# A planner with prices for VectorE beside GpSimd, ten staging tiles, another order of the first loads, and no idle matmuls

## The chip, the core and the metric

The kernel runs on one core of one Trainium2 chip. The core has TensorE (PE: matmuls; PEld: its weight loads), VectorE (DVE), ScalarE (ACT), GpSimd (POOL) and SyncE (SP), whose queue issues nearly all DMA transfers of this kernel. Each engine runs its instructions in the order in which they are written; an instruction that waits holds up all that stand behind it on its engine. The metric is the time of one execution in device microseconds, lower is better.

## What is computed

Chunked attention over 4 batches, 8 heads, 768 positions and 64 values each, followed by a gated feed-forward layer:

```python
for c in range(nc):                       # 24 chunks of 32 queries
    # keys of the chunk, 16 before, 8 behind, and 8 memory keys
    scores = scale * matmul(q_c, k_full.T)
    a = softmax(scores)
    out[:, :, c_start:c_end] = matmul(a, v_full)
x = out in [B, S, H * D]                  # 4 x 768 x 512
h = maximum(x @ w_in, 0.0)                # 512 -> 1024
u, v = h[..., :512], h[..., 512:]
v_n = (v - mean(v)) / sqrt(var(v) + 1e-6)
v_s = einsum('ts,bsd->btd', w_spatial, v_n) + b_spatial
return (u * v_s) @ w_out                  # 512 -> 512
```

## The kernel before

**A planner writes the order.** The program first lists its operations with `plan.op(engine, us, ...)`: an engine, a price in us, the keys it reads and writes, and a rank. `Plan.order` then simulates the engines with these prices: again and again it takes, over all engines, the operation that could start first, and among those of one engine with equal start the lowest rank. Ring sizes (`sizes`) bound how many tiles of a name are alive. What comes out is one fixed order for each engine; the prices and ranks are used for nothing else.

**First phase, to about 227 us.** 24 units `i` of four chunks go through `attend(i)`: copies of the keys to `kmain` (L377, ScalarE), a burst on TensorE (L395) of scores S(i) into half 0 of `sx` and of value products A(i) of unit i − 1 into half 1, 16 matmuls per pair of heads each; then the maximum `mx` (L445), the subtraction into `p` (L449), the exponential (L453, ScalarE), the sum `den` and its reciprocal `rec` (L458–L461); the transposes of `p` into `pt` (L475) and of the normalised values `xs` (L430) into `xt` (L490). `xt` is split into a high part (L495, ScalarE, a cast to fp32r) and a low part (L499, VectorE, the difference). `sx`, `p`, `xs` and `pT` have one buffer each. Values come with four transfers per unit into `vmain`.

Between the units stand the matmuls of the feed-forward layer, each product as three (high by high, low by high, high by low, L528–L530): `ffn_v` (512 wide, twelve per 128 positions), then `ffn_u` (384 wide, twelve per block). The v half is normalised and written to DRAM (`vn_far`), the u half too (`u_far`).

**w_in** arrives as 64-bit floats, in eight pieces (c, part) of 128 x 512, each over one of four `big` buffers: ScalarE scales (L824, L829), VectorE shifts (L833, L834), POOL adds (L839), ScalarE casts the high part (L853), VectorE or POOL subtracts the low part (L857). Part 1 serves v, part 0 serves u. w_out's and w_spatial's pieces go the same or a like way later. SP issues all these loads in program order where `seq=True`, and SP also waits there for a free buffer.

**Idle matmuls.** `keep_warm` puts four 512-wide matmuls (L543) on TensorE as soon as the first high part of w_in is there; their result is not used.

**Second phase.** For each batch b, `spatial(b)` multiplies v_n by w_spatial and `ffn_o(b)` multiplies the gated result by w_out, both as a product of seven steps instead of eight (`product`): sums and differences of quarters `sm` (L651, VectorE), high parts `op` (L664, ScalarE), low parts (L667, VectorE), blocks of matmuls (L689; L683 adds the bias), results taken to SBUF (L731, L780), joined (L737) and gated with u (L745, POOL). Both are generators that yield after each step: `spatial` goes p1 p2 p6 p5 p7 p4 p3, `ffn_o` p1 p6 p5 p7 p4 p3 p2. The loop over b takes one step of spatial(b), then ffn_o(b − 1), then the rest of spatial(b).

## Time and profile before

| what | value |
|---|---|
| median of 3 runs | 395.51 us (395.07 to 395.77) |
| profiled execution, its span | 395.85 us, 394.1 us |
| TensorE busy | 368.4 us, 93%, 3428 matmuls |
| VectorE busy | 281.0 us, 71% |
| ScalarE busy | 210.2 us, 53% |
| GpSimd busy | 157.5 us, 40% |
| DMA over the span | 64.93 MB, 165 GB/s |
| chain that ended last | 80% on TensorE, 8% on VectorE |

Busy times are of one profiled execution; the span runs from the first to the last recorded instruction. In a timeline row, the bracket at the end gives how long the engine had been idle and what released it. A row of a transfer on SP's queue gives when it was issued.

### The profile page before, as it was taken

To read this page: it belongs to the slowest core of one execution; us is meant where nothing else is said; L and a number is where in the kernel's file an instruction comes from. 1 tells how busy PE (TensorE), PEld (TensorE's weight loads), DVE (VectorE), ACT (ScalarE), POOL (GpSimd) and SP (SyncE) were. 2 spreads that over 40 slices of the span, in tenths; PEclk is the share of its full clock that TensorE was granted. 3 is DMA by queue.
4 is the path that set the end of the run, shared out by engine and by line. 5 is a ranking of instruction groups with operands and counts; after the bars stand their busy time and mean duration, and the time that the engine had idled before them with its cause. 6 is when DMAs were issued, how large, how long until landed. Compare 5 with 4: busy or idle time off the path is not lost.

```text
span 394.1 us, 8707 instructions
## 1 busy us (share of the span) xinstructions
PE 368.4 (93%) x3428; PEld 335.0 (85%) x3428; DVE 281.0 (71%) x465; ACT 210.2 (53%) x368; POOL 157.5 (40%) x161
## 2 busy tenths in 40 slices
PE   1659899999999999999999998899999999999996
PEld 1437688898898988988889898799999999999996
DVE  7975965756856558866575499978956794788594
ACT  4765646575456557464434475438434734473361
POOL 8433762193621177601012968770226033403520
PEclk9999999999999999999999999999999999999999
DMA  8998567676575683786603768403640562040014
GB/s 231 309 232 210 129 202 230 183 251 185 182 219 160 235 221 112 211 223 206 187 29 136 257 237 278 136 25 121 210 153 0 162 233 89 0 175 27 2 40 161
DMA packets 47356, 64.93 MB, mean 165 GB/s; under 512 B 4434, under 2 KB 38866, under 8 KB 47316
## 3 DMA queue, kind: packets, MB, share of 16 engines
q1 hardware_dynamic: 46900, 64.25, 53.5%
q8 instruction: 27, 0.44, 0.5%
q10 hardware_dynamic: 416, 0.13, 0.1%
q14 instruction: 13, 0.11, 0.1%
HBM read 45.49 MB, written 18.87 MB: 163 GB/s over the span
## 4 chain that ended last, share of the span: by engine, by line
PE 80%; DVE 8%; issue 2%; ACT 2%; POOL 1%; ACTq 0%
PE y L689 16%; PE f L689 12%; PE f L528 12%; PE sx L395 11%; PE f L530 11%; PE f L529 11%; PE xt L490 3%; PE pt L475 3%; DVE wout L857 2%; DVE sm L651 2%; DVE op L667 2%; POOL ug L745 1%; DVE st L737 1%; ACT op L664 1%; DVE st L834 0%
## 5 line engine op out<-in xcount | busy, mean ns | idle before, releaser
L745 POOL TENSOR_TENSOR ug<-st,ug 128x384 f32<-128x384 f32 x32 | 43.8, 1380 | 79.6 <-DVE st L737 62.0
L528 PE MATMUL f<-x,win_h 128*128 128x384 f32 x128 | 45.8, 358 | 0.0
L574 POOL TENSOR_TENSOR rstd<-ve,mhalf 128x1 f32<-128x1 f32 x24 | 13.5, 562 | 77.4 <-DVE ve L570 75.7
L664 ACT CAST op<-sm 128x768 fp32r<-128x768 f32 x32 | 26.3, 837 | 32.5 <-DVE sm L651 29.9
L530 PE MATMUL f<-x,win_h 128*128 128x384 f32 x128 | 43.2, 338 | 0.0
L529 PE MATMUL f<-x,win_l 128*128 128x384 f32 x128 | 43.0, 336 | 0.0
L528 PE MATMUL f<-win_h,x 128*128 128x512 f32 x96 | 41.6, 433 | 0.0
L689 PE MATMUL y<-wsp,op 128*128 128x384 f32 x192 | 39.5, 341 | 2.0 <-ACT st L731 1.2
L395 PE MATMUL sx<-kmain,q 128*32 128x128 f32 x768 | 28.5, 294 | 11.3 <-ACT kmain L377 9.3
L377 ACT COPY kmain<-k 64x640 f32<-64x640 f32 x48 | 34.7, 724 | 6.8 <-DMA k<-in_k_dram 4.0
L530 PE MATMUL f<-win_l,x 128*128 128x512 f32 x96 | 38.2, 398 | 0.0
L529 PE MATMUL f<-win_h,x 128*128 128x512 f32 x96 | 38.1, 397 | 0.0
L430 DVE TENSOR_TENSOR xs<-sx,rec 128x512 f32<-128x512 f32 x24 | 16.6, 690 | 29.7 <-PE sx L395 29.7
L667 DVE TENSOR_TENSOR op<-sm,op 128x768 fp32r<-128x768 f32 x32 | 33.6, 1056 | 5.3 <-ACT op L664 4.9
L689 PE MATMUL y<-wout,op 128*128 128x256 f32 x288 | 36.2, 280 | 0.8 <-ACT ot L780 0.7
L395 PEld LDWEIGHTS sx<-kmain,q 128*32 128x32 f32 x768 | 21.5, 117 | 18.2 <-POOL vmain L369 10.1
L689 PEld LDWEIGHTS y<-wsp,op 128*128 128x128 f32 x192 | 33.9, 188 | 3.2 <-ACT st L731 1.9
L689 PEld LDWEIGHTS y<-wout,op 128*128 128x128 f32 x288 | 34.9, 188 | 1.2 <-ACT ot L780 0.9
L369 POOL COPY vmain<-memv 8x1024 f32<-8x1024 f32 x22 | 23.8, 1083 | 17.6 <-PE sx L395 16.2
L689 PE MATMUL f<-wsp,op 128*128 128x384 f32 x144 | 29.4, 339 | 1.5 <-DVE op L667 1.5
L599 ACT ACTIVATE uo<-f 128x384 f32<-128x384 f32 x32 | 15.6, 490 | 26.8 <-PE f L530 17.7
L689 PE MATMUL f<-wout,op 128*128 128x256 f32 x216 | 27.3, 280 | 0.0
(100 smaller groups left out, 833.4 us busy)
## 6 DMA issues: line engine op xcount, KB each, us to landing
vmain<-in_v_dram SPq DMA_DIRECT2D x48, 128.0 KB
vn_far<-st SPq DMA_DIRECT2D x24, 256.0 KB
u_far<-uo SPq DMA_DIRECT2D x32, 192.0 KB
vr<-vn_far SPq DMA_DIRECT2D x8, 768.0 KB
ug<-u_far SPq DMA_DIRECT2D x16, 384.0 KB
q<-in_q_dram SPq DMA_DIRECT2D x11, 512.0 KB
out_dram<-ot SPq DMA_DIRECT2D x36, 128.0 KB
vmain<-in_v_dram SPq DMA_DIRECT2D x47, 96.0 KB
```

What stands on the lines that cost most here:

```text
L369: {"DVE": nc.vector, "POOL": nc.gpsimd}[eng].tensor_copy(to, of)
L377: nc.scalar.copy(kmain[i % NK][rows, :, r, :, 0:CH], k_of(i)[rows].rearrange("p t (c s) -> p t c s", s=CH))
L395: nc.tensor.matmul(o, w_, m, start=True, stop=True, skip_group_check=True)
L430: nc.vector.tensor_tensor(xs, t_["sx", i][:, 1], rec.unsqueeze(3).broadcast_to([P, T, 2, D]), op=ALU.mult)
L528: nc.tensor.matmul(o, lh, rh, start=(j == 0), stop=False)
L529: nc.tensor.matmul(o, ll, rh, start=False, stop=False)
L530: nc.tensor.matmul(o, lh, rl, start=False, stop=(j == len(pairs) - 1))
L599: op("ACT", act(HT), lambda: nc.scalar.activation(alloc("uo", i, [P, HT], F32), t_["f", n], AF.Relu), r=[("f", n)], w=[("uo", i)], rank=rank)
L664: nc.scalar.copy(half(0), of())
L667: nc.vector.tensor_tensor(half(1), of(), half(0).bitcast(F32), op=ALU.subtract)
L689: nc.tensor.matmul(o, x, y, start=first and m == 1 and not (seed and bank != "x"), stop=m == 3 * chunks, skip_group_check=True)
L745: nc.gpsimd.tensor_tensor(g, t_[st(x)], g, op=ALU.mult)
```

## The change

The planner gets a flag `shared` on VectorE operations with two inputs in SBUF. Such an operation that starts while POOL is busy is priced longer, by up to a factor of 1.75, and a POOL operation that starts beside a flagged one by up to 1.4. Some prices are set anew. The ring `st` has ten tiles instead of eight. The first values and the second pair of queries and keys are loaded between the w_in pieces; the four part-0 pieces come last with ranks 15 to 18, and their low parts go to VectorE instead of POOL. The four idle matmuls are gone. In the second phase, batches 1 and 2 take two steps of `spatial(b)` before `ffn_o(b - 1)` starts.

```diff
@@ class Plan @@
-    def op(self, eng, us, fn, r=(), w=(), rank=0.0, mb=0.0, tail=0.0, after=None, alone=False, drag=1.0):
+    def op(self, eng, us, fn, r=(), w=(), rank=0.0, mb=0.0, tail=0.0, after=None, alone=False, drag=1.0, shared=False):
...
-        lone = 0.0
+        lone = both = 0.0
...
+            beside, pace = {"DVE": (free["POOL"] if shared else 0.0, 1.75), "POOL": (both, 1.4)}.get(e, (0.0, 1.0))
+            if beside > t:
+                us += min((beside - t) * (1 - 1 / pace), us * (pace - 1))
...
+            if shared:
+                both = t + us
@@ the rings @@
-    sizes = {"f": 3, "sx": 1, "pt": 2, "xt": 1, "y": 5, "st": 8, "big": 4, "uo": 2, "x": 2, "vm": 3,
+    sizes = {"f": 3, "sx": 1, "pt": 2, "xt": 1, "y": 5, "st": 10, "big": 4, "uo": 2, "x": 2, "vm": 3,
@@ burst, softmax, flip, ffn_v @@
-                us += 0.7
+                us += 0.88 if "s" in what else 0.6
-        op("DVE", dve(512) + 0.36, den, r=[("p", i)], w=[("rec", i)], rank=rank + 0.6)
+        op("DVE", dve(512) + 0.43, den, r=[("p", i)], w=[("rec", i)], rank=rank + 0.6, shared=True)
-            op("PE", 0.45, turn, r=[("p", i)], w=[("pt", i)], rank=rank, tail=0.25)
+            op("PE", 0.47, turn, r=[("p", i)], w=[("pt", i)], rank=rank, tail=0.25)
...
-        op("DVE", 1.05, stat, r=[k_], w=[("ve", i)], rank=rank)
+        op("DVE", 1.08, stat, r=[k_], w=[("ve", i)], rank=rank, shared=True)
@@ idle matmuls @@
-    def keep_warm(c, passes, rank):
-
-        n = ("w", c)
-
-        def go():
-            o = alloc("f", n, [P, DH], F32, psum=True)
-            for _ in range(passes):
-                nc.tensor.matmul(o, win_h[:, c, DH:DH + P], win_h[:, c, DH:], start=True, stop=True)
-        op("PE", passes * 0.43, go, r=[("win", c, 1, "h")], w=[("f", n)], rank=rank, tail=0.25)
...
-        if i == 0:
-            for c in range(1):
-                keep_warm(c, 4, 50.0 + c)
@@ product: total, left; split @@
-            op(sum_eng, dve(W) if sum_eng == "DVE" else pool_(W), go, r=keys, w=[sm], rank=rank)
+            op(sum_eng, dve(W) if sum_eng == "DVE" else pool_(W), go, r=keys, w=[sm], rank=rank,
+               shared=sum_eng == "DVE")
-            op("DVE", dve(W), low, r=[*keys, (*ok, "h")], w=[(*ok, "l")], rank=rank)
+            op("DVE", dve(W), low, r=[*keys, (*ok, "h")], w=[(*ok, "l")], rank=rank, shared=True)
...
@@ the order of the first loads @@
     w_in_part(0, 1, 5.0 + 0, 2.0 + 0, "DVE")
     w_in_part(1, 1, 5.0 + 1, 2.0 + 1, "DVE")
-    w_in_part(2, 1, 5.0 + 2, 2.0 + 2, "DVE")
-    w_in_part(3, 1, 5.0 + 3, 2.0 + 3, "DVE")
     load_v(0)
     load_qk(1)
-    w_in_part(0, 0, 25.0 + 0, 15.0 + 0, "POOL")
+    w_in_part(2, 1, 5.0 + 2, 2.0 + 2, "DVE")
     load_v(1)
-    w_in_part(1, 0, 25.0 + 1, 15.0 + 1, "POOL")
+    w_in_part(3, 1, 5.0 + 3, 2.0 + 3, "DVE")
     load_v(2)
-    w_in_part(2, 0, 25.0 + 2, 15.0 + 2, "POOL")
-    w_in_part(3, 0, 25.0 + 3, 15.0 + 3, "POOL")
+    w_in_part(0, 0, 15.0 + 0, 15.0 + 0, "DVE")
+    w_in_part(1, 0, 15.0 + 1, 15.0 + 1, "DVE")
+    w_in_part(2, 0, 15.0 + 2, 15.0 + 2, "DVE")
+    w_in_part(3, 0, 15.0 + 3, 15.0 + 3, "DVE")
@@ the second phase @@
             spatials.append(spatial(b))
-            next(spatials[b])
+            for _ in range((1, 2, 2, 1)[b]):
+                next(spatials[b])
```

Names in the rows below: an engine's rows are line, operation, destination, sources and shape; lines of the changed kernel are shifted by about five (L395 is now L400, L528 L533, L667 L663, L857 L853).

TensorE, the third to the ninth group of its work, before (`pt` and `xt` are transposes, `kmain` rows are scores, `vmain` rows value products, `f` rows with `x` the v products):

```order
L475 MATMUL pt<-ident,p 128x128 x4
L543 MATMUL f<-win_h 128x512 x4
L395 MATMUL sx<-vmain,pT 32x128 x16
L475 MATMUL pt<-ident,p 128x128 x4
L490 MATMUL xt<-ident,xs 128x128 x4
L395 MATMUL sx<-kmain_144,q 32x128 x16
L528 MATMUL f<-win_h,x 128x512
L529 MATMUL f<-win_h,x 128x512
L530 MATMUL f<-win_l,x 128x512
```

and now:

```order
L400 MATMUL sx<-vmain,pT 32x128 x16
L480 MATMUL pt<-ident,p 128x128 x4
L495 MATMUL xt<-ident,xs 128x128 x4
L533 MATMUL f<-win_h,x 128x512
L534 MATMUL f<-win_h,x 128x512
L535 MATMUL f<-win_l,x 128x512
L533 MATMUL f<-win_h,x 128x512
L534 MATMUL f<-win_h,x 128x512
L535 MATMUL f<-win_l,x 128x512
L400 MATMUL sx<-kmain_144,q 32x128 x16
L400 MATMUL sx<-vmain,pT 32x128 x16
L400 MATMUL sx<-kmain_145,q 32x128 x16
```

The idle matmuls are gone, two groups of three v products come ahead of the scores of unit 2, and the scores of unit 3 (`kmain_145`) follow directly behind the value products of unit 2.

VectorE at the same place (`p` of unit 1, `xs` of unit 0, `x` the low part of tile 0), before:

```order
L833 TENSOR_SCALAR st<-st 128x512
L834 SCALAR_TENSOR_TENSOR st<-big,st 128x512
L857 TENSOR_TENSOR win_l<-st,win_h 128x512
L458 TENSOR_REDUCE den<-p 128x8
L459 TENSOR_TENSOR den<-den,eps 128x8
L461 RECIPROCAL rec<-den 128x8
L857 TENSOR_TENSOR win_l<-st,win_h 128x512
L833 TENSOR_SCALAR st<-st 128x512
L834 SCALAR_TENSOR_TENSOR st<-big,st 128x512
L430 TENSOR_TENSOR xs<-sx,rec 128x512
L857 TENSOR_TENSOR win_l<-st,win_h 128x512
L499 TENSOR_TENSOR x<-xt,x 128x4x128
```

and now:

```order
L454 TENSOR_TENSOR p<-sx,mx 128x512
L435 TENSOR_TENSOR xs<-sx,rec 128x512
L463 TENSOR_REDUCE den<-p 128x8
L464 TENSOR_TENSOR den<-den,eps 128x8
L466 RECIPROCAL rec<-den 128x8
L853 TENSOR_TENSOR win_l<-st,win_h 128x512
L504 TENSOR_TENSOR x<-xt,x 128x4x128
L829 TENSOR_SCALAR st<-st 128x512
L830 SCALAR_TENSOR_TENSOR st<-big,st 128x512
L450 TENSOR_REDUCE mx<-sx 128x8
L454 TENSOR_TENSOR p<-sx,mx 128x512
L435 TENSOR_TENSOR xs<-sx,rec 128x512
```

`xs` of unit 0 stood ten rows behind `p` of unit 1 and now stands right behind it.

SP's queue behind the second pair of queries and keys, before:

```order
L256 DMA big<-in_moe_w_in_dram 128x1024
L256 DMA vmain<-in_v_dram 32x4x256
L256 DMA vmain<-in_v_dram 24x4x256
L256 DMA vmain<-in_v_dram 32x4x256
L256 DMA vmain<-in_v_dram 24x4x256
L256 DMA big<-in_moe_w_in_dram 128x1024 x2
L256 DMA vmain<-in_v_dram 32x4x256
L256 DMA vmain<-in_v_dram 24x4x256
L256 DMA vmain<-in_v_dram 32x4x256
L256 DMA vmain<-in_v_dram 24x4x256
L256 DMA q<-in_q_dram 128x4x256
L256 DMA k<-in_k_dram 128x4x272
```

and now:

```order
L261 DMA big<-in_moe_w_in_dram 128x1024
L261 DMA vmain<-in_v_dram 32x4x256
L261 DMA vmain<-in_v_dram 24x4x256
L261 DMA vmain<-in_v_dram 32x4x256
L261 DMA vmain<-in_v_dram 24x4x256
L261 DMA big<-in_moe_w_in_dram 128x1024 x4
L261 DMA vmain<-in_v_dram 32x4x256
L261 DMA vmain<-in_v_dram 24x4x256
L261 DMA vmain<-in_v_dram 32x4x256
L261 DMA vmain<-in_v_dram 24x4x256
L261 DMA q<-in_q_dram 128x4x256
```

The last two w_in pieces stand ahead of the values of unit 3 in both; now there are four pieces in that place, since two were moved back.

VectorE at the start of the second phase (`op` rows are the low parts for the seven steps, `wout` rows the low parts of w_out, the shift rows belong to w_out as well), before:

```order
L667 TENSOR_TENSOR op<-sm,op 128x768
L857 TENSOR_TENSOR wout<-big,wout 128x256
L651 TENSOR_TENSOR sm<-vr,sm 128x768
L857 TENSOR_TENSOR wout<-big,wout 128x2x256
L857 TENSOR_TENSOR wout<-st,wout 128x2x256
L833 TENSOR_SCALAR st<-st 128x512
L834 SCALAR_TENSOR_TENSOR st<-big,st 128x512
L737 TENSOR_TENSOR st<-f,st 128x384
L857 TENSOR_TENSOR wout<-st,wout 128x2x256
L737 TENSOR_TENSOR st<-f,st 128x384
L667 TENSOR_TENSOR op<-sm,op 128x768
L857 TENSOR_TENSOR wout<-big,wout 128x256
```

and now:

```order
L663 TENSOR_TENSOR op<-sm,op 128x768
L646 TENSOR_TENSOR sm<-vr,sm 128x768
L663 TENSOR_TENSOR op<-sm,op 128x768
L829 TENSOR_SCALAR st<-st 128x512
L830 SCALAR_TENSOR_TENSOR st<-big,st 128x512
L853 TENSOR_TENSOR wout<-big,wout 128x256
L733 TENSOR_TENSOR st<-f,st 128x384
L646 TENSOR_TENSOR sm<-vr 128x768
L733 TENSOR_TENSOR st<-f,st 128x384
L853 TENSOR_TENSOR wout<-big,wout 128x2x256
L663 TENSOR_TENSOR op<-sm,op 128x768
L853 TENSOR_TENSOR wout<-st,wout 128x2x256 x2
```

Before, the two `op<-sm` rows are the low parts of p6 and p5. Now there are three, of p6, p5 and p7: p5's stands right behind p6's, ahead of all w_out low parts, and p7's stands behind two of them instead of five.

More of the change, by code (lines that the diff above doesn't have):

```diff
@@ L60, in op @@
         begun -= deps
-        self.ops.append((eng, us, fn, deps, rank, mb, tail, held, begun, alone, drag))
+        self.ops.append((eng, us, fn, deps, rank, mb, tail, held, begun, alone, drag, shared))
         return n
@@ L103, in order @@
             (t, _, n), e = best
-            _, us, _, _, _, mb, tail, held, _, alone, drag = ops[n]
+            _, us, _, _, _, mb, tail, held, _, alone, drag, shared = ops[n]
+            beside, pace = {"DVE": (free["POOL"] if shared else 0.0, 1.75), "POOL": (both, 1.4)}.get(e, (0.0, 1.0))
+            if beside > t:
+                us += min((beside - t) * (1 - 1 / pace), us * (pace - 1))
             for s in held:
@@ L500, in low @@
                                         op=ALU.subtract)
-            op("PE", 0.45, turn_x, r=[("xs", j)], w=[("xt", j)], rank=rank - 0.5, tail=0.25)
+            op("PE", 0.47, turn_x, r=[("xs", j)], w=[("xt", j)], rank=rank - 0.5, tail=0.25)
             op("ACT", act(512) - 0.04, high, r=[("xt", j)], w=[("x", n, tt, "h")], rank=rank - 0.5)
@@ L858, in split @@
         op("ACT", act(n), high, r=reads, w=[(*w, "h") for w in writes], rank=rank)
-        op(eng, pool_(n) if eng == "POOL" else dve(n), low, r=[*reads, *[(*w, "h") for w in writes]], w=writes, rank=rank)
+        op(eng, pool_(n) if eng == "POOL" else dve(n), low, r=[*reads, *[(*w, "h") for w in writes]], w=writes, rank=rank,
+           shared=eng == "DVE")
     def w_in_part(c, part, rank, load_rank, sub_eng):
```

## The prediction

> **What bounds the kernel now.** I first read the busy time of each engine in five stretches of the span. A row is: stretch, its length, then busy time and count for PE, PEld, DVE, ACT and POOL, the granted clock, the DMA share and GB/s.
>
> ```profile
> 0.00:60.00 60.00, 41.77 (x472) 31.80 (x473) 45.98 (x81) 35.34 (x60) 32.83 (x42) 1.00 0.82 220
> 60.00:227.00 167.00, 167.00 (x1893) 145.83 (x1892) 105.60 (x217) 91.08 (x155) 61.82 (x73) 1.00 0.63 189
> 227.00:270.00 43.00, 38.90 (x226) 37.16 (x225) 39.47 (x45) 23.46 (x44) 30.21 (x23) 1.00 0.44 153
> 270.00:370.00 100.00, 100.00 (x682) 100.00 (x681) 72.74 (x98) 50.19 (x92) 27.92 (x21) 1.00 0.34 115
> 370.00:394.10 24.10, 20.68 (x164) 20.16 (x162) 17.26 (x26) 10.11 (x21) 4.76 (x4) 1.00 0.24 82
> ```
>
> TensorE sets the time. It never rests in 60–227 and 270–370, so 267 of 394.1 us can only be lengthened by reordering. What can be won lies in its idle time: 18.2 us at the start (60 − 41.77), 4.1 at the change of phase (43 − 38.90), 3.4 at the end. The waits of TensorE (waiter, what released it: total, times, longest) say for what:
>
> ```profile
> PE sx L395 <- ACT kmain L377: 9.3, 2, 7.7
> PE xt L490 <- DVE xs L430: 3.5, 2, 2.9
> PE f L689 <- DVE op L667: 1.5, 1, 1.5
> PE y L689 <- ACT st L731: 1.2, 2, 0.8
> ```
>
> The 7.7 is the first input, and the diff leaves it where it is. The 2.9 and the last two rows are late small work of VectorE and ScalarE: an order can mend these. The order of the tail, after 370, is not altered.
>
> **The start.** This is the timeline from 16 to 49 us (start, duration, engine, operation).
>
> ```profile
> 16.05 1.30 POOL L839 TENSOR_TENSOR st<-st,big 128x512 uint32<-128x512 uint32 x1 [2.01 <-DVE st L834]
> 16.33 1.57 DVE L857 TENSOR_TENSOR win_l<-st,win_h 128x512 fp32r<-128x512 f32 x1 [0.41 <-ACT win_h L853]
> 16.35 2.07 PE L543 MATMUL f<-win_h 128*128 128x512 f32 x4 [1.75 <-ACT win_h L853]
> 17.82 0.68 DVE L449 TENSOR_TENSOR p<-sx,mx 128x512 f32<-128x512 f32 x1
> 18.55 1.93 PE L395 MATMUL sx<-vmain,pT 128*32 128x128 f32 x32
> 23.67 0.68 DVE L430 TENSOR_TENSOR xs<-sx,rec 128x512 f32<-128x512 f32 x1
> 24.41 1.11 PE L490 MATMUL xt<-ident,xs 128*128 128x128 f32 x4 [2.87 <-DVE xs L430]
> 26.45 0.68 DVE L499 TENSOR_TENSOR x<-xt,x 128x512 fp32r<-128x512 f32 x1
> 27.10 1.94 PE L395 MATMUL sx<-kmain,q 128*32 128x128 f32 x32 [1.58 <-ACT kmain L377]
> 27.78 0.43 DVE L833 TENSOR_SCALAR st<-st 128x512 uint32<-128x512 uint32 x1 [0.65 <-ACT st L824]
> 28.25 0.69 DVE L834 SCALAR_TENSOR_TENSOR st<-big,st 128x512 uint32<-128x512 uint32 x1
> 34.80 0.69 DVE L458 TENSOR_REDUCE den<-p 128x8 f32<-128x512 f32 x1 [0.16 <-ACT p L453]
> 35.72 0.20 DVE L461 RECIPROCAL rec<-den 128x8 f32<-128x8 f32 x1
> 35.78 1.08 PE L395 MATMUL sx<-kmain,q 128*32 128x128 f32 x32
> 43.18 0.68 DVE L499 TENSOR_TENSOR x<-xt,x 128x512 fp32r<-128x512 f32 x1
> 48.82 0.34 PE L530 MATMUL f<-x,win_h 128*128 128x384 f32 x1
> ```
>
> Taking away the four idle matmuls costs nothing at once: the first value product (18.55) stood behind them until 18.42 and behind `p` until 18.50, and now can run at about 15.3, when its own inputs are there. It ends at 17.2. VectorE's next op, still the `p` at 17.82, is then followed directly by `xs` (18.5 to 19.2) instead of 23.67. The transpose takes 1.11 and is queued behind one other; the cast and the low part follow, so `x` of tile 0 is whole at about 22.5 instead of 27.13, **4.6 earlier**. But that is not the gain, since something else is late next. The scores of unit 3 share the one `sx` buffer and must wait for `xs` of unit 1. The scores of unit 2, which follow two value groups in the new order, I place at 24.7–26.6, their value products at 27.4–29.3, `xs` of unit 1 until 30.75: scores of unit 3 at 30.8, still **5.0 earlier** than 35.78. From there to the low part of `x` for tile 2, VectorE has twelve steps in the new order: eight of 0.68 or so, one den (34.80 to 35.92: 1.1) and three shifts (27.78 to 28.94: 1.16), 10.0 together, so 40.8 if it never waits; two short waits on transposes (0.5 each) and one stretch like the 1.57 at 16.33 (0.9 over the 0.68) make it 42.7. Before, that step ended at 43.86: 1.2 earlier. Behind it the old order has 5.1 us to the end of the first six u products (49.0), with one value product of 1.08 that the new order does not have there; the new one needs 4.1, ends at 46.8, and is 2.2 ahead, but owes that value product and a set of transposes (about 0.5 more). Net **0.6**; before also idled about 1 us more between there and 60 (rests of 0.2 to 0.3 ahead of its bursts), of which I count half: **gain 1.1**. Bounds: without wait and stretch 3.0, with two stretches more −0.7.
>
> The low parts of the four part-0 pieces go to VectorE: two of the twelve steps. The 14.0 us that VectorE idles in 0–60 cover the rest; without cover each costs its 0.68. Ten staging tiles cost nothing in time.
>
> The clock: before, a burst took 1.93 at 18.55 and still 1.94 at 27.10, and 1.08 at 35.78, though the granted column says 1.00 throughout. So the idle matmuls did not speed up what followed them, and I price their loss at nothing beyond their own 2.07, which is in the sum. By the Trainium skill (TensorE: Matmul & The Clock Gate, What's actually happening) the array runs at half clock until it has been busy through one window of some 3.4 us, and goes back after an idle one. In the new order work is unbroken from about 21.9 to 26.6, so by that rule unit 2's value product and unit 3's scores could already run fast, and the estimate from it would be up to 1.2 us better; the rows here cannot time that window.
>
> SP's queue: the w_in pieces (2,0) and (3,0) now stand ahead of unit 3's values and of the queries and keys for units 4 and 5. Each needs a `big` buffer, freed by a POOL addition. I place those two at 27 and 35, so what is queued behind them issues in 35–40:
>
> ```profile
> 33.85 0.39 SPq L256 DMA_DIRECT2D q<-in_q_dram  x1
> 44.67 1.46 ACT L377 COPY kmain<-k 64x640 f32<-64x640 f32 x2
> ```
>
> It was 33.85, and the key copies ran at 44.67; 40 plus 3 of transfer still comes in time. Priced at nothing, with a rival below for the case that this cover is gone.
>
> **Between 60 and 227** nothing can be won. The new costs pull some softmax steps closer together, so that one or two products may wait for a late input; the nearest row is the second `xt` wait, 3.5 − 2.9 = 0.6. I take **a loss of 0.5**, bounds 0 and 1.2.
>
> **The change of phase.** Timelines of TensorE and of VectorE:
>
> ```profile
> 244.09 0.34 PE L683 MATMUL f<-bias,ones 128*128 128x384 f32 x1
> 252.18 1.22 PE L689 MATMUL y<-wsp,op 128*128 128x384 f32 x6
> 254.31 1.31 PE L689 MATMUL y<-wsp,op 128*128 128x384 f32 x6 [0.38 <-ACT st L731]
> 256.99 1.32 PE L689 MATMUL y<-wsp,op 128*128 128x384 f32 x6 [0.84 <-ACT st L731]
> 258.66 1.22 PE L689 MATMUL f<-wsp,op 128*128 128x384 f32 x6
> 260.25 1.22 PE L689 MATMUL f<-wsp,op 128*128 128x384 f32 x6
> 265.32 2.27 PE L689 MATMUL y<-wout,op 128*128 128x256 f32 x18
> 268.25 2.37 PE L689 MATMUL y<-wout,op 128*128 128x256 f32 x18 [0.67 <-ACT ot L780]
> 270.46 1.80 PE L689 MATMUL f<-wout,op 128*128 128x256 f32 x14
> ```
>
> ```profile
> 244.73 1.29 DVE L667 TENSOR_TENSOR op<-sm,op 128x768 fp32r<-128x768 f32 x1
> 249.68 0.95 DVE L667 TENSOR_TENSOR op<-sm,op 128x768 fp32r<-128x768 f32 x1
> 250.54 2.07 DVE L667 TENSOR_TENSOR op<-vr,op 128x768 fp32r<-128x768 f32 x1
> ```
>
> A half step of nine matmuls is 1.59 where nothing waits (258.66 to 260.25), 1.76 with its bias matmul. From 244.09 to 252.18 run two with bias and one without: 8.09 against 5.11, **2.98 lost** because the low parts of p5 (until 246.02) and p7 (until 250.63) are late. Then 2.13, 2.68 and 1.67 where 1.59 is due: **1.7 lost**. The first step of the output product is followed after 2.93, the next after 2.21: **0.7 lost**. Together 5.4. In the new order p5's low part comes before the shifts and w_out's low parts, and p7's before the last two w_out pairs: I place them about 9 and 4 us ahead of need. p2 of batch 1, moved ahead of the output product, gives that product's first step 3.2 us more slack. What is late next is that same p2: its low part stands behind three w_out low parts, is due at about 260.8 and done at 261.2, a stall of 0.4, and up to 1.5 if it is stretched as the 2.07 is over the 0.95. Its second vr load waits only for p4's low part (about 248) and lands some 10 us early. I count 1.4 of the 5.4 as staying: **gain 4.0**, bounds 5.4 (nothing late) and 1.5.
>
> The plan now prices a VectorE operation beside POOL at 1.75 of its pace. At 16.33 it overlapped POOL for 1.02 and took 0.89 more; the plan's formula gives 1.02 × (1 − 1/1.75) = 0.44. The Trainium skill (SBUF — State Buffer, the section SBUF: two separate sides) says that the two share a port pair as an exclusive lock for the whole instruction, the loser blocked; that gives 1.02, which the row's 0.89 is nearer to, and it speaks against an order built on a softer price.
>
> **Sum:** 1.1 − 0.5 + 4.0 = 4.6 less than the profiled execution's 395.85 (span 394.1, 1.75 around it): 391.25. The median is 0.34 under that execution, so about **390.9**.
>
> **Rivals.**
> (a) The start's lead is eaten. For it: VectorE's chain binds from 30.8 on, and two more stretches of 0.9 cancel it. Against: POOL has lost four low parts there. Gain 4.0 − 0.5 − 0.7 = 2.8: 392.7.
> (b) VectorE is the bound at the change of phase. For it: 39.47 busy of 43; if its work stays in that stretch and does not shrink, TensorE gains at most the 3.5 it idles, and with stretches only 1.5. Against: it has 37% free before 227, and p5's low part can move there. Gain 1.1 − 0.5 + 1.5 = 2.1: 393.4.
> (c) The order does not do what its prices say: each stall turns up one step later. For it: the 0.44 against 0.89. Then the gain is 0.3 or so: 395.2.
> (d) Slower: SP's queue behind the two w_in pieces. If the additions that free the `big` buffers come at 41 or later instead of 35, then unit 3's values and the keys land after TensorE wants them at 47, and each further us is one us of idle TensorE. It decides over the forecast only if 6 us over: 390.9 + 6 = 396.9. For it: 0.82 DMA share in 0–60, and POOL, 32.8 of 60 busy there, has long rests only while it waits for VectorE. Against: that takes 12 us more than I placed.
>
> **How the numbers follow.** Forecast 0.50 (its own range 389 to 392.2), (a) 0.16, (b) 0.14, (c) 0.09, (d) 0.11. The measurement can tell about 0.2%, 0.8 us, from no change: forecast, (a) and (b) are faster, 0.80; (c) is the same, 0.09; (d) slower, 0.11. The range leaves out (c) and (d), 0.20, and takes in the good bounds: 388.6 to 394.2.
>
> **What would show it.** `xs` of unit 0 right behind `p` near 18.5; scores of unit 3 near 31; the first six u products ending near 47; no TensorE wait over 0.5 for the low part of `op` between 240 and 256; one wait near 261 of 0.4 to 1.5; 60 to 370 otherwise full. It is wrong if TensorE waits for key copies or values between 44 and 56, if idle appears inside 60–227, or if TensorE's idle in 227–270 stays above 3.

## The result, and the profile after

The changed kernel is slower: 399.81 us (median of 9 runs, 397.38 to 400.85) against 395.44 us for the kernel before (9 runs, 394.66 to 396.35), a ratio of 1.0098, 95% interval 1.0070 to 1.0125. The forecast was 390.9. The runs fall into two groups, near 398 and near 400.5; why is part of the answer below. The profiled execution took 400.64 with a span of 398.9, so it is one of the upper group.

This is the busy time by stage after the change, columns as before:

```profile
0.00:60.00 60.00, 42.28 (x453) 33.25 (x457) 44.69 (x78) 35.14 (x59) 27.07 (x36) 0.94 0.85 213
60.00:227.00 167.00, 166.46 (x1911) 143.91 (x1900) 106.40 (x221) 89.84 (x153) 61.06 (x73) 1.00 0.64 186
227.00:270.00 43.00, 36.71 (x203) 35.33 (x202) 40.31 (x45) 24.84 (x43) 34.88 (x25) 0.99 0.54 176
```

The first thing to see is not a busy share but the granted clock: 0.94 in the first 60 us. Then VectorE's and GpSimd's load between 227 and 270: 40.31 instead of 39.47, and 34.88 instead of 30.21. TensorE's waits after the change (waiter, what released it: total, times, longest):

```profile
PE sx L400 <- ACT kmain L382: 7.9, 1, 7.9
PE f L685 <- DVE op L663: 4.0, 1, 4.0
PE y L685 <- DVE op L663: 2.3, 2, 1.6
PE f L534 <- DVE x L504: 2.2, 2, 2.0
```

The 2.9 for `xs` is gone, as forecast. A wait of 4.0 for a low part is new, and it is longer than any that was removed.

To find where the time went I compared the start of the same piece of work in both traces:

```profile
234.26 0.34 PE L683 MATMUL y<-bias,ones 128*128 128x384 f32 x1
```

```profile
235.53 0.34 PE L679 MATMUL y<-bias,ones 128*128 128x384 f32 x1
...
253.90 1.14 PE L685 MATMUL y<-wsp,op 128*128 128x384 f32 x5 [1.55 <-DVE op L663]
...
256.99 1.22 PE L685 MATMUL f<-wsp,op 128*128 128x384 f32 x6
...
264.95 0.34 PE L685 MATMUL f<-wsp,op 128*128 128x384 f32 x1
269.30 1.97 PE L685 MATMUL f<-wsp,op 128*128 128x384 f32 x5 [4.01 <-DVE op L663]
273.90 2.27 PE L685 MATMUL y<-wout,op 128*128 128x256 f32 x18
```

The first fence is the first matmul of the second phase before. The second shows it after, then a wait for p4's low part, the start of p3, the stall of p2 of batch 1 and the start of the output product. p3 began at 258.66 before, the output product at 265.32. So:

| stretch | before | after | difference |
|---|---|---|---|
| start to the second phase | 234.3 | 235.5 | +1.3 |
| second phase to p3 of batch 0 | 24.4 | 21.5 | −2.9 |
| from there to the output product | 6.7 | 16.9, of which 3.2 is p2, moved here | +7.1 |
| output product to the end | 128.8, of which 3.2 is p2 | 125.0 | −0.6 |
| span | 394.1 | 398.9 | +4.8 |

The changed order does gain 2.9 at the steps of batch 0, as the prediction worked out. It loses 7.1 right behind them and 1.3 at the start.

**The loss behind p3.** VectorE's timeline after the change:

```profile
260.63 1.03 DVE L663 TENSOR_TENSOR op<-vr,op 128x768 fp32r<-128x768 f32 x1
261.59 1.49 DVE L853 TENSOR_TENSOR wout<-st,wout 128x512 fp32r<-128x512 f32 x1
263.00 0.55 DVE L733 TENSOR_TENSOR st<-f,st 128x384 f32<-128x384 f32 x1
264.97 1.74 DVE L646 TENSOR_TENSOR sm<-ug 128x768 f32<-128x768 f32 x1 [1.42 <-POOL ug L741]
266.75 1.63 DVE L646 TENSOR_TENSOR sm<-sm,ug 128x768 f32<-128x768 f32 x1
268.30 0.94 DVE L663 TENSOR_TENSOR op<-vr,op 128x768 fp32r<-128x768 f32 x1
```

The `op<-vr` at 260.63 is the low part of p1 of batch 1. The one of p2, due at 265.1, comes at 268.30: two sums `sm<-ug` of the output product stand ahead of it on VectorE, and the first of them waits 1.42 for a gate of GpSimd while everything behind it waits too. GpSimd after and before:

```profile
257.52 1.20 POOL L878 TENSOR_TENSOR st<-big,st 128x256 f32<-128x256 f32 x1
258.68 1.01 POOL L741 TENSOR_TENSOR ug<-st,ug 128x384 f32<-128x384 f32 x1
259.66 1.19 POOL L878 TENSOR_TENSOR st<-big,st 128x256 f32<-128x256 f32 x1
260.81 6.75 POOL L741 TENSOR_TENSOR ug<-st,ug 128x384 f32<-128x384 f32 x5
```

```profile
254.71 1.20 POOL L881 TENSOR_TENSOR st<-big,st 128x256 f32<-128x256 f32 x1
257.00 6.80 POOL L745 TENSOR_TENSOR ug<-st,ug 128x384 f32<-128x384 f32 x5 [1.09 <-DVE st L737]
```

The run of five gates starts at 260.81 instead of 257.00, since the last sums of w_out (L878) end at 260.8 instead of 255.9. The order that brings the low parts of p5 and p7 forward has pushed the conversion of w_out back on both engines. Of the 3.8 us, 1.3 are the later start of the phase; counted from that start the gates are 2.5 later, while TensorE is 2.9 earlier at p3.

**The clock.** A row per stretch of the start, first of the changed kernel, then of the one-step experiment below, whose start has the same order:

```profile
20.00:30.20 10.20, 7.55 (x77) 5.07 (x75) 4.63 (x10) 5.99 (x10) 1.29 (x1) 1.00 1.01 236
30.20:33.60 3.40, 3.01 (x38) 2.65 (x39) 2.79 (x7) 1.52 (x3) 0.37 (x1) 0.52 0.15 57
33.60:44.00 10.40, 8.36 (x66) 6.05 (x65) 8.51 (x13) 7.82 (x14) 4.30 (x4) 0.99 0.69 170
44.00:47.40 3.40, 3.40 (x11) 2.92 (x10) 3.25 (x8) 2.82 (x6) 2.64 (x3) 0.50 1.10 234
```

```profile
30.20:33.60 3.40, 3.33 (x67) 2.67 (x70) 2.91 (x7) 2.85 (x5) 0.85 (x1) 1.00 0.11 42
33.60:44.00 10.40, 8.42 (x55) 6.35 (x45) 9.65 (x17) 7.87 (x15) 5.45 (x6) 1.00 0.66 170
44.00:47.40 3.40, 3.40 (x49) 2.91 (x47) 3.27 (x7) 1.53 (x3) 2.85 (x3) 1.00 1.04 234
```

In the profiled execution of the changed kernel the clock is at half for 3.4 us from 30.3 and again from 44.0, each time behind a stretch with 2.0 to 2.7 us of rest (10.20 − 7.55 and 10.40 − 8.36). In the other execution the same rests bring no drop. The matmuls' own times agree; these are the scores of unit 3, behind the same wait of 1.49, first in the changed kernel, then in the one-step experiment:

```profile
30.59 1.94 PE L400 MATMUL sx<-kmain,q 128*32 128x128 f32 x32 [1.49 <-ACT p L458]
30.11 1.08 PE L400 MATMUL sx<-kmain,q 128*32 128x128 f32 x32 [1.49 <-ACT p L458]
```

Six traces in this document are of kernels with this start in the same order and nothing in the rests. Two show both drops (the changed kernel, and the one with fewer sums on GpSimd), one shows the first drop alone (p2's low part first), three show none (one step, idle matmuls at p2, eight staging tiles). With none the second phase starts at 231.6 to 232.1, with one at 234.0, with two at 235.0 and 235.5. Before, it started at 234.3, and at 233.9 in the trace of the move alone, whose start is the old one. So the start is better than before by about 2 us, or worse by 1. The same happens behind the wait of 4.0:

```profile
265.30:269.30 4.00, 0.00 (x1) 0.00 (x1) 3.97 (x4) 1.90 (x4) 2.26 (x2) 1.00 0.00 0
269.30:272.60 3.30, 3.30 (x10) 3.30 (x11) 2.02 (x3) 0.73 (x1) 0.00 (x0) 0.50 0.00 0
```

### The profile page after: what moved, and what is told of

The parts are those of the page before. It is cut to its first block, busy times and chain, and to the rows that moved or that the text cites. A ratio compares the mean times of both kernels' runs of the same rounds, so it can differ in the third digit from the quotient of the medians.

```text
span 398.9 us, 8690 instructions
## 1 busy us (share of the span) xinstructions
PE 370.6 (93%) x3424; PEld 337.1 (85%) x3424; DVE 284.6 (71%) x469; ACT 210.4 (53%) x368; POOL 155.5 (39%) x157
## 5 line engine op out<-in xcount | busy, mean ns | idle before, releaser
L533 PE MATMUL f<-x,win_h 128*128 128x384 f32 x128 | 46.9, 366 | 0.0
L535 PE MATMUL f<-x,win_h 128*128 128x384 f32 x128 | 43.4, 339 | 0.0
L533 PE MATMUL f<-win_h,x 128*128 128x512 f32 x96 | 41.4, 431 | 0.7 <-ACT x L500 0.7
L569 POOL TENSOR_TENSOR rstd<-ve,mhalf 128x1 f32<-128x1 f32 x24 | 14.9, 619 | 65.4 <-DVE ve L565 64.7
L400 PE MATMUL sx<-kmain,q 128*32 128x128 f32 x768 | 29.3, 299 | 11.4 <-ACT kmain L382 7.9
L400 PEld LDWEIGHTS sx<-kmain,q 128*32 128x32 f32 x768 | 22.2, 119 | 18.7 <-issue 13.3
L663 DVE TENSOR_TENSOR op<-sm,op 128x768 fp32r<-128x768 f32 x32 | 33.2, 1039 | 3.6 <-ACT op L660 3.3
L685 PE MATMUL f<-wsp,op 128*128 128x384 f32 x144 | 30.7, 349 | 4.0 <-DVE op L663 4.0
L727 ACT COPY st<-y 128x384 f32<-128x384 f32 x32 | 15.3, 478 | 32.1 <-PE y L685 30.7
L685 PEld LDWEIGHTS f<-wsp,op 128*128 128x128 f32 x144 | 26.5, 196 | 4.5 <-DVE op L663 4.3
```

The lines of the kernel that those rows point to most:

```text
L400: nc.tensor.matmul(o, w_, m, start=True, stop=True, skip_group_check=True)
L533: nc.tensor.matmul(o, lh, rh, start=(j == 0), stop=False)
L535: nc.tensor.matmul(o, lh, rl, start=False, stop=(j == len(pairs) - 1))
L663: nc.vector.tensor_tensor(half(1), of(), half(0).bitcast(F32), op=ALU.subtract)
L685: nc.tensor.matmul(o, x, y, start=first and m == 1 and not (seed and bank != "x"), stop=m == 3 * chunks, skip_group_check=True)
L727: op("ACT", act(HT), lambda: nc.scalar.copy(alloc("st", st(x)[1], [P, HT], F32), t_[bank]), r=[bank], w=[st(x)], rank=rank)
```

## The experiments

Two theories of the loss at the phase change stood against each other (M: the move of p2 is the loss; Q: GpSimd's gates and the two sums are), and two of the start (C: the clock falls in the rests; D: VectorE's chain sets it anyway). Ratios are against the kernel before on the same chip, with 95% intervals. Where a kernel's runs fall into groups, its median depends on how many runs fell into each, so a difference of two such medians is uncertain by 1 us or more; there the traces are the better measure, above all the time from the start of the second phase to the end, which leaves the start out.

**One step instead of two.**

```diff
-            for _ in range((1, 2, 2, 1)[b]):
+            for _ in range((1, 1, 1, 1)[b]):
```

> The changed kernel with one step of spatial before the output product for every batch, as before the change; all else stays. Theory M (the move itself is the loss): p2's low part of batch 1 is no longer due before the output product, so the wait of 4.01 at 265 and the cold clock behind it (1.6) go: about 5.5 less, near 394. Theory Q (the loss sits in the queues: GpSimd's five gates run late, from 260.8 to 267.6, and VectorE's sums for the output product wait for them): the wait moves to the output product's second step and is 2 to 4 us there, so at most 3 less, 396.5 to 398.5.

399.43 us, ratio 1.0084 (1.0056 to 1.0111), next to no gain on the changed kernel. The wait went to the output product's second step, as Q said, and the clock fell behind it too:

```profile
266.61 0.38 PE L685 MATMUL y<-wout,op 128*128 128x256 f32 x1 [2.84 <-ACT op L660]
267.60 3.26 PE L685 MATMUL y<-wout,op 128*128 128x256 f32 x17 [0.61 <-DVE op L663]
```

It is a little over Q's range. The move of p2 is not the cause; M falls.

**p2's low part first.**

```diff
@@ total @@
-               shared=sum_eng == "DVE")
+               shared=sum_eng == "DVE", after=t_.get(("p2 low", b + 1)) if kind == "o" else None)
@@ left @@
-            op("DVE", dve(W), low, r=[*keys, (*ok, "h")], w=[(*ok, "l")], rank=rank, shared=True)
+            n = op("DVE", dve(W), low, r=[*keys, (*ok, "h")], w=[(*ok, "l")], rank=rank, shared=True)
+            if kind == "s" and name == "a12":
+                t_["p2 low", b] = n
```

> The changed kernel, with the two sums of the output product kept behind p2's low part of the next batch on VectorE; the move of p2 stays. Theory Q (p2's low part was late only because it stood behind two sums that wait for GpSimd's gates): the wait of 4.01 shrinks to under 1, the clock does not drop at 269, 4 to 5.5 less than the changed kernel, 394.5 to 396. Theory M: what is late is the cast of p2's values or VectorE as a whole, the wait stays above 2.5, less than 2 us are won.

396.19 us, ratio 1.0004 (0.9983 to 1.0025), 3.6 under the changed kernel by the medians, a little short of Q's 4 to 5.5. From the start of the second phase to the end it takes 160.0 instead of 163.4, so 3.4 of it is there. TensorE's wait at p2:

```profile
264.28 1.15 PE L687 MATMUL f<-wsp,op 128*128 128x384 f32 x5 [0.52 <-DVE op L663]
```

0.52 instead of 4.01, and no drop of the clock there. Place and cause of the stall are as Q has them.

**Fewer sums on GpSimd.** The eight sums of w_out on GpSimd are replaced by fills with zeros, so this kernel leaves out the right side of the output product.

```diff
+                if name == "wout":
+                    nc.gpsimd.memset(part(x, j), 0.0)
+                    return
                 {"DVE": nc.vector, "POOL": nc.gpsimd}[sum_eng].tensor_tensor(part(x, j), in0(), in1(), op=o)
```

> The changed kernel, same order on every engine; left out are the eight sums of w_out's pieces on GpSimd, which are fills with zeros instead (the output product's right side is wrong). Theory Q (GpSimd is late with the gates because w_out's sums stand ahead of them, and VectorE's sums and p2's low part wait behind): the gates end before 262, the wait of 4.0 falls under 1, no cold stretch near 269, 4 to 7 less than the changed kernel, 393 to 396. Rival (the cast of p2's values at 263.8 or its load is late by itself): the wait stays above 2.5, less than 2.5 us won.

393.9 us, ratio 0.9956 (0.9935 to 0.9977), 5.9 under the changed kernel. The five gates run from 255.28 to 262.44, and the other waits for `op` in that stage are gone. But the wait at p2 is 2.09, not under 1, and the clock falls behind it: the two sums still stand ahead of p2's low part. So the stall of 4.01 needs both, GpSimd's lateness and the place in VectorE's queue: with the gates early 2.09 of it is left, with the sums behind the low part 0.52, though the gates are as late there as before this mend (25.3 us behind the start of the phase in both). The fills also press less on VectorE (between 240 and 264 the four low parts `wout<-st` take 0.88 on the mean instead of 1.21), so this run can't say how much of the 5.9 is the queue and how much the contention.

**The move alone, and the prices alone,** on the kernel before.

```diff
-            next(spatials[b])
+            for _ in range((1, 2, 2, 1)[b]):
+                next(spatials[b])
```

> The kernel before, with the move of p2 alone. Theory Q (p2's low part stands behind the two sums on VectorE here too, but GpSimd's gates run from 257.0 as before, not from 260.8): a wait of 0 to 1.5 ahead of p2, the output product's wait of 0.7 gone: 394.5 to 396.5. Rival M (the move alone is the loss): a wait of 3 to 4 and a cold stretch, 398 to 400.

396.08 us, ratio 1.0022 (1.0011 to 1.0033): a wait of 1.22 ahead of p2, no drop of the clock, inside Q's range. For the prices the changed kernel was given back the old loads, the idle matmuls, eight tiles and one step:

```diff
-                us += 0.7
+                us += 0.88 if "s" in what else 0.6
...
+            beside, pace = {"DVE": (free["POOL"] if shared else 0.0, 1.75), "POOL": (both, 1.4)}.get(e, (0.0, 1.0))
```

> The kernel before, with the new prices alone: old loads, idle matmuls, eight staging tiles, one step. Theory P (the prices bring the 2.9 that the changed kernel gains between the first step and p3 of batch 0, and lose it where the output product's sums wait for GpSimd): the first five steps run 2 to 3 us faster, then a wait of 2 to 4 ahead of the output product's second step: 395 to 397.5. Rival: the prices cost nothing, the move of p2 does: 392.5 to 394.

399.73 us, ratio 1.0105 (1.0084 to 1.0126), over the range of both. By the median the prices alone make the whole loss. In the one trace, of the fastest of the four runs (398.13), the second phase takes 163.2, as in the changed kernel; what the other runs lost beyond it, up to 2.2, no trace shows. Their order gains at batch 0 (p1 of batch 1 begins at 257.9 there, 261.8 before) and loses behind it:

```profile
268.11 0.39 PE L695 MATMUL y<-wout,op 128*128 128x256 f32 x1 [3.25 <-ACT op L670]
269.10 3.81 PE L695 MATMUL y<-wout,op 128*128 128x256 f32 x17 [0.61 <-DVE op L673]
```

**Idle matmuls in the rests of the start.**

```diff
@@ burst, value products @@
+                def idle(n):
+                    for _ in range(n if i == 2 else 0):
+                        mm(t_["xt", 0].rearrange("p t n -> p (t n)"), win_h[:, 0, DH:DH + P], win_h[:, 0, DH:])
+                idle(3)
                 for t, c, rows in tiles:
                     mm(sx[rows, 1, t], pT[:, t, rows], vt[:, t, :, c])
+                idle(6)
@@ group @@
+                for _ in range(8 if n == 2 and j == 0 else 0):
+                    nc.tensor.matmul(o, win_h[:, 0, DH:DH + P], win_h[:, 0, DH:], start=True, stop=True)
```

> The changed kernel with 17 idle matmuls of 512 columns more (3 ahead of and 6 behind the value product of unit 2, 8 ahead of the third v block), all in places where TensorE waited: 27 to 30.6 and 40.4 to 42.5. Theory C (the two rests cool the clock, 30.2 to 33.4 and 44 to 47.4, at 1.4 and 1.7 us): the granted clock stays 1.00 up to 60, the first six u products end 1.5 to 3 earlier, the whole is 1.5 to 3 less. Theory D (VectorE's chain sets the start, the clock is only seen beside it): the clock stays up but u products and the whole move by less than 0.5; or they get later by the idle matmuls' own time.

397.68 us, ratio 1.0050 (1.0030 to 1.0070), 2.1 under the changed kernel; its four runs lie within 1.4 us, the nine of the changed kernel within 3.5. The same holds over all the kernels here: the five with the rests filled spread by 1.4 to 2.3, the six with the same start unfilled by 3.4 to 4.4. The clock is 1.00 over the whole start, and the second phase begins at 231.7:

```profile
30.20:33.60 3.40, 3.32 (x71) 2.57 (x59) 2.59 (x7) 2.53 (x5) 1.17 (x1) 1.00 0.06 23
44.00:47.40 3.40, 3.40 (x48) 2.95 (x47) 3.26 (x8) 2.27 (x5) 2.56 (x3) 1.00 1.01 196
```

Theory C holds for the start, 3.8 us between this trace and that of the changed kernel, with its two drops, at the same point. The stall at p2 stayed, with 4.0.

**Idle matmuls at p2 only.**

```diff
+                    for _ in range(20 if (kind, b, name, cols.start) == ("s", 1, "p2", 0) else 0):
+                        nc.tensor.matmul(o, half(0)[:, 0, cols], right(bi, 0, 0), start=True, stop=True)
```

> The changed kernel, same order, with 20 idle matmuls of 384 columns (3.5 us) directly ahead of p2's matmuls of batch 1, where TensorE waited 4.0 and then ran cold for 3.2. If the cold stretch is set by the rest alone, p2's low part still comes at 269.2 of the trace, but the clock stays up: 1.4 to 1.8 less than the changed kernel, and no wait over 1 there. If the clock drop costs nothing by itself (VectorE is late behind it too), less than 0.5.

398.11 us, ratio 1.0040 (1.0012 to 1.0067), 1.7 less than the changed kernel; from the start of the second phase to the end it takes 161.6 instead of 163.4. The clock stays at 1.00 there:

```profile
261.25 3.70 PE L679 MATMUL f<-wsp,op 128*128 128x384 f32 x20
264.78 0.34 PE L687 MATMUL f<-wsp,op 128*128 128x384 f32 x1
265.63 1.15 PE L687 MATMUL f<-wsp,op 128*128 128x384 f32 x5 [0.51 <-DVE op L663]
...
268.73 4.37 PE L687 MATMUL y<-wout,op 128*128 128x256 f32 x36
```

From p2's place to the output product it takes 7.5 (261.25 to 268.73) instead of 8.95 (264.95 to 273.90): of the 5.8 over p2's own 3.2, some 1.5 were the clock and the rest the wait for the low part. The ten runs are still in two groups, four near 395.2 and six near 398.4, so the groups come from elsewhere; the profiled execution was of the lower group and had no drop between 27 and 60. The mean granted clock on record for each run does not tell the groups apart (0.991 to 1.000 in the lower, 0.978 to 1.000 in the upper), so that the groups are the drops of the start rests on the traces and on the spreads above.

**The old start in the changed kernel,** with the idle matmuls of before.

```diff
+    w_in_part(2, 1, 5.0 + 2, 2.0 + 2, "DVE")
+    w_in_part(3, 1, 5.0 + 3, 2.0 + 3, "DVE")
     load_v(0)
     load_qk(1)
-    w_in_part(2, 1, 5.0 + 2, 2.0 + 2, "DVE")
+    w_in_part(0, 0, 25.0 + 0, 15.0 + 0, "POOL")
...
```

> The changed kernel with the old order of the first loads, part-0 low parts on GpSimd with the old ranks and the four idle matmuls; prices, staging tiles and the second phase as changed. The changed kernel reached the second phase 1.2 us later than the kernel before. Theory C: the old start has no such cold stretches, so the second phase begins 1 to 2 earlier and the whole is 1 to 2 less, 398 to 399 beside 399.8. Theory D: the retuned prices, not the start, cost the 1.2; nothing changes (within 0.5).

399.02 us, ratio 1.0086 (1.0068 to 1.0103), 0.8 less than the changed kernel: between the two. Its trace reaches the second phase at 233.4 and has a drop of its own from 41.8 to 45.2, behind two rests of 1.35 and 0.78, so the old start with the new prices isn't free of them, as C had assumed.

**The new start in the kernel before,** old prices.

```diff
-    w_in_part(2, 1, 5.0 + 2, 2.0 + 2, "DVE")
-    w_in_part(3, 1, 5.0 + 3, 2.0 + 3, "DVE")
     load_v(0)
     load_qk(1)
-    w_in_part(0, 0, 25.0 + 0, 15.0 + 0, "POOL")
+    w_in_part(2, 1, 5.0 + 2, 2.0 + 2, "DVE")
...
```

> The kernel before with the new order of the first loads, part-0 low parts on VectorE and no idle matmuls; old prices, eight staging tiles, one step. Theory C: the first six u products end 2 to 5 earlier than 49.0, 2 earlier at the second phase if the clock holds, level or late where it drops at the rests near 30 and 41; the second phase keeps its old waits: 393 to 396, spread over more than 1.5 us from run to run. Theory D (the new start is a loss in itself): 396.5 or more in every run.

405.75 us, ratio 1.0265 (1.0247 to 1.0283): ten over C's range. D's "396.5 or more in every run" holds (404.12 to 406.56), with a loss far above the one that it was to explain. TensorE waits once for `pT`:

```profile
45.81 1.93 PE L395 MATMUL sx<-vmain,pT 128*32 128x128 f32 x32 [6.80 <-ACT pT L478]
```

The copy to `pT` stands on ScalarE behind six casts and scalings of w_in and runs at 45.17, and from 42.5 to 49.4 the clock is at half. There is a second cold stretch from 257.6 to 264.4, behind a wait of 2.53 at the change of phase, and a third from 274.2. With the old prices the new loads are a loss in themselves; with the order that the new prices make they bring the second phase 2 us forward where the clock holds. Neither can be judged alone.

**Without the idle matmuls,** the kernel before otherwise.

```diff
-        if i == 0:
-            for c in range(1):
-                keep_warm(c, 4, 50.0 + c)
```

> The kernel before, without its four idle matmuls, nothing else. As predicted on record: they cost and bring nothing; the value product of unit 1 runs 3 us earlier and waits for nothing less behind it, the time is within 0.8 of before. Rival (they keep the clock up): the clock becomes full later than 32, and the time is 1 to 2.5 more.

395.40 us, ratio 0.9996 (0.9986 to 1.0007). The prediction's price of nothing is right for this part, in the kernel before.

**Eight staging tiles** in the changed kernel.

```diff
-    sizes = {"f": 3, "sx": 1, "pt": 2, "xt": 1, "y": 5, "st": 10, "big": 4, "uo": 2, "x": 2, "vm": 3,
+    sizes = {"f": 3, "sx": 1, "pt": 2, "xt": 1, "y": 5, "st": 8, "big": 4, "uo": 2, "x": 2, "vm": 3,
```

> The changed kernel with eight staging tiles instead of ten: TensorE's and GpSimd's order are the same, VectorE's differs in twelve rows behind p3 of batch 0. As predicted on record, the tiles are worth nothing: within 1 of the changed kernel. Rival: the ten tiles carry part of the loss or of a gain: over 1.5 away.

397.69 us (six runs, 395.82 to 400.25), ratio 1.0060 (1.0026 to 1.0094). The interval overlaps that of the changed kernel (1.0070 to 1.0125). The medians differ by 2.1, but with the two groups of the start in both this tells nothing sure: unclear. Its profiled execution had no drop between 27 and 60, and 3.48 of wait at p2; its second phase takes 164.1 us, so nothing there says that the two tiles more are the loss.

**Both mends together:** the 17 idle matmuls, and p2's low part first (the diffs of both, above).

> The changed kernel with both mends: the 17 idle matmuls in the two rests, and the two sums behind p2's low part. If the loss is the sum of the two causes (C: the clock after the rests, 3.7 in the profile of the changed kernel; Q: the wait of 4.0 and its cold stretch), the second phase begins near 232, no clock falls below 1.00 before the tail, and the time is 393 to 394, 0.4 to 0.6% under the kernel before. If one gain is given back later (a wait that was covered by the other), it is 395 or more.

**393.97 us**, ratio 0.9966 (0.9954 to 0.9978) to the kernel before, 9 runs from 393.2 to 395.0: faster than both kernels. TensorE's waits behind 227 in it:

```profile
PE y L694 <- DVE op L670: 2.3, 2, 1.6
PE f L694 <- DVE op L670: 0.5, 1, 0.5
PE y L694 <- ACT ot L785: 0.5, 1, 0.5
```

The two causes add up: 399.81 − 393.97 = 5.8; alone they gave 2.1 and 3.6. One trace of each kernel, split at the first matmul of the second phase:

| kernel | second phase begins | from there to the end |
|---|---|---|
| before | 234.3 | 159.8 |
| changed | 235.5 | 163.4 |
| one step | 232.1 | 163.0 |
| the prices alone | 233.1 | 163.2 |
| idle matmuls in the rests | 231.7 | 164.2 |
| p2's low part first | 234.0 | 160.0 |
| both mends | 232.2 | 159.9 |

So what the kernel with both mends has over the kernel before is the start. In the second phase it is level: the 2.9 gained up to p3 are given back, 2.0 from p3 to the output product and 1.0 behind it.

**Three further tries at the phase change.** In the first, with both mends, the gate has its true price:

```diff
-            op("POOL", 1.05, go, r=[st(x)], w=[(*u, p)], rank=rank)
+            op("POOL", 1.4, go, r=[st(x)], w=[(*u, p)], rank=rank)
```

> As the one with both mends, but with the planner's price of a gate on GpSimd at 1.4 instead of 1.05 (the trace shows 1.36 on the mean). Theory Q says that the wrong price lets the plan put sums ahead of what they delay: with the true price 0.3 to 1.5 less, by the output product's sums. Rival: p4's low part still stands behind two shifts, so its wait of 1.6 stays and the time is within 0.5 of the one with both mends.

396.20 us, ratio 1.0021 (1.0010 to 1.0032), 2.2 over the kernel with both mends. p4's wait stays at 1.56, and its waits for `op` at the `y` bank are 5.0 in all, six of them, instead of 2.3. A truer price gave a worse order. In the second, with one step and the idle matmuls, the flag is taken off the second phase:

```diff
-            op(sum_eng, dve(W) if sum_eng == "DVE" else pool_(W), go, r=keys, w=[sm], rank=rank,
-               shared=sum_eng == "DVE")
+            op(sum_eng, dve(W) if sum_eng == "DVE" else pool_(W), go, r=keys, w=[sm], rank=rank)
...
-            op("DVE", dve(W), low, r=[*keys, (*ok, "h")], w=[(*ok, "l")], rank=rank, shared=True)
+            op("DVE", dve(W), low, r=[*keys, (*ok, "h")], w=[(*ok, "l")], rank=rank)
...
-           shared=eng == "DVE")
+           shared=eng == "DVE" and writes[0][0] != "wout")
```

> The changed kernel with the idle matmuls in the two rests, one step, and the price for VectorE beside GpSimd taken off the second phase's sums and low parts and off w_out's. Theory P (the loss is the second phase's prices, the gain is the start): no wait over 2 ahead of the output product's steps, no cold stretch after 60, 392.5 to 394.5. Rival: any order that brings the low parts of p5 and p7 forward delays GpSimd's gates, whatever the price: a wait of 2 to 4 near 265 again, 396 to 398.

396.66 us, ratio 1.0035 (1.0023 to 1.0046). No wait at 265, but one of 2.67 for ScalarE's `st`, which ends at 254.95, with a cold clock behind it: the stall has found another place. The rival's range holds the time but not the place, and theory P holds neither. In the third, with both mends, w_out's eight sums go to VectorE:

```diff
-        right_hand("wout", c, HN, halves(zu), halves(zd), [ku, *end], [kd, *end], dst, rank, "POOL", "DVE")
+        right_hand("wout", c, HN, halves(zu), halves(zd), [ku, *end], [kd, *end], dst, rank, "DVE", "DVE")
```

> The kernel with both mends (17 idle matmuls, p2's low part first), with w_out's eight sums on VectorE instead of GpSimd. Theory Q (GpSimd's lateness and its stretching of VectorE cost the rest of the phase change): the gates end by 262, p4's wait of 1.6 shrinks, 391.5 to 393.5. Rival B (VectorE, 39 to 41 busy of 43, is the bound there, and eight sums of 0.43 more make every later part later): 394.5 to 397.

395.11 us, ratio 0.9982 (0.9968 to 0.9996), 1.1 over the kernel with both mends:

```profile
248.34 0.44 PE L694 MATMUL y<-wsp,op 128*128 128x384 f32 x1 [2.45 <-ACT op L667]
249.75 1.97 PE L694 MATMUL y<-wsp,op 128*128 128x384 f32 x5 [0.97 <-DVE op L670]
```

GpSimd falls from 35.16 to 22.80 busy between 227 and 270, but p7's parts are late now, and the clock is at half from 248.8 to 255.7. Rival B's range holds the time; that VectorE is full was not measured apart from the order that it got.

## Why the prediction was wrong

**The change of phase.** The step that failed is the sentence that what is late next is p2's low part, "behind three w_out low parts, is due at about 260.8 and done at 261.2, a stall of 0.4". What was done at 261.7 is the low part of p1 of that batch, with a stall of 0.73. p2's came at 269.2: in VectorE's new order the output product's two sums are ahead of it. The sums need gates of GpSimd, and GpSimd appears in no term of that step. Its 30.21 of 43 busy stood in the quoted row; where a part of VectorE's work is brought forward, w_out's conversion goes back, and the gates behind it on GpSimd by 3.8, 1.3 of it the later start. What was right is that p5 and p7 no longer wait (2.98), and that the output product's wait of 0.7 goes (0.6). In place of the 1.4 that it counted as staying, 8.8 stayed or came new: 1.7 at batch 0, nearly all of it p4's low part (placed at "about 248", done at 253.9, a wait of 1.55), and 7.1 behind p3: 4.0 of wait and 1.7 of cold clock at p2, 1.2 at p1 and 0.1 at p3. Rival (c), a stall that turns up one step later, had the right mechanism and too small a size: 395.2 at 0.09. A rival in which a stall comes back larger than those removed was missing. And mending the stall at p2 does not bring the forecast 4.0 back: with it the second phase is level with the kernel before.

**The start.** The gain of 1.1 was, without a drop of the clock, 1.8 to 2.6 (the second phase at 231.6 to 232.1 in three traces with this start, 233.9 and 234.3 with the old one): the mechanism was right and the size a little low. In the one-step trace the scores of unit 3 start at 30.1 (placed at 30.8), and VectorE's twelve steps take 10.4 instead of 11.9, since the 1.9 of waits and stretch that the sum added came to 0.4. What failed is the step on the clock. It asked what the four idle matmuls do for the clock, rightly found nothing, and did not ask what the clock does in the rests that the new order has: scores of unit 3 waiting until 30.6, the third v block waiting for `x` at 42.5. Both waits stand in the prediction's own working, as stations of VectorE's chain. One drop cost about 2 in the traces (234.0 with one, 232 with none), two cost 3 to 4 (235.0 and 235.5).

The Trainium skill (TensorE: Matmul & The Clock Gate, What's actually happening) states both directions, that the array goes back to half clock after an idle window of some 3.4 us and that the windows run free. The prediction quoted the way back to half clock too, and worked out only the way up. The traces agree with the length: the drops last 3.4, or twice that (6.8 from 264.5 with the 17 idle matmuls in the start), and the two of the changed kernel's start begin 13.7 apart, four times 3.4. But a whole window without work is not needed: 1.9 us of rest in the 3.4 ahead of 44.0 were enough.

**SP's queue** (rival d) did nothing: the changed kernel's key copies ran at 48.9 and TensorE never waited for keys or values in 44–56. **Between 60 and 227** TensorE idled 0.54, where a loss of 0.5 was forecast. **The last phase** gained 0.6 of the 0.7 that was expected of the output product's wait. Two signs that the prediction named for its being wrong were there: idle inside 60–227, and TensorE's idle in 227–270 above 3 (43 − 36.71 = 6.3). Its lower bound of 388.6 comes out of no sum that it shows; its good bounds together give 3.0 − 0 + 5.4 = 8.4, or 387.1.

**The softer price of VectorE beside GpSimd** is too low at the one row that the prediction worked out (0.44 against 0.89), and no run tells what a harder one would do; the true price of the gate made things worse.

## What to carry to other kernels

When an order is changed to bring late work forward, list what it is put ahead of, on every engine in turn, down to the one that looks idle enough: there the stall comes back, and it can be longer than the one that was removed. Look at each rest of TensorE of about 2 us or more with the clock in mind: it can cost another 1.5 to 2 behind it, in some executions only, so a start with rests makes a kernel's runs fall into groups. Idle matmuls in the rests themselves can end that: here 17 of them were worth 2.1 by the medians, while the four ahead of the old start were worth nothing. Compare traces by phase as well as by the total: a gain in one phase can hide that another is only level. A planner's prices are judged by the order they give, not by how true they are.

## What was not expected of the hardware

The granted clock fell for 3.4 us where TensorE had rested about 2 us out of 3.4, and in three of six executions with the same order of instructions there it did not. Filling the rests ended both the drops and most of the spread: 1.4 us between runs instead of 3.5. At the change of phase it was sharper: in the ten traces with a wait of TensorE of 2.09 or more (up to 4.01) a drop came with it each time, and in the seven where the longest wait was 1.57 or less none did. A sum of two counts as well: 1.53 and 0.61 close together, in the new start with the old prices, had a drop behind them. The granted clock of a profile is not complete, though: before the change it reads 1.00 at 18.55, where a burst took 1.93 that takes 1.08 later, and in the trace with idle matmuls at p2 it reads 0.50 from 19 to 25.
